# A fused attention and two feed-forward layers: five square groups on GpSimd, sums by rows first, the first fold in quarters

## The chip, the cores and the metric

The kernel runs on one core of a Trainium2 chip. The metric is device time in microseconds (us) from one launch to its end. Engines are named as in the profile: PE is TensorE (PEld its weight loads), DVE is VectorE, ACT is ScalarE, POOL is GpSimd, SP is SyncE, which here only issues DMAs.

## What is computed

```python
qn = q / (np.linalg.norm(q, axis=1, keepdims=True) + 1e-06)     # q, k, v: 1 x 6016 x 256, f32
kn = k / (np.linalg.norm(k, axis=1, keepdims=True) + 1e-06)
s = kn.transpose(0, 2, 1) @ qn / tau                            # 256 x 256
a = np.exp(s - s.max(-1, keepdims=True)); a /= a.sum(-1, keepdims=True) + 1e-09
x = v @ a                                                       # 6016 x 256
h = x @ w_in1;  x = (h * np.cos(h)) @ w_out1                    # d_ff = 2048, weights f64
h = x @ w_in2;  x = (h / (1 + np.exp(-h))) @ w_out2
```

The norms run over the 6016 tokens, so each of the 512 columns of q and k has one sum of squares. `v @ a @ w_in1` is computed as `v @ (a @ w_in1)`: the attention matrix is folded into the first weight, and v goes straight through the folded weight.

## The kernel before

**Opening.** q and k come in 25 groups (`GROUPS`: two of one chunk, 22 of two, one of one; a chunk is 128 tokens x 512 columns) into seven buffers, loaded by SP in order. For each group PE adds k^T q to the score matrix S, in two halves S[0] and S[1] (`emit_scores`, L617, two passes of 256 columns per chunk and half; four groups, `FINE`, go in another form at L606). ACT squares the group (L649). DVE adds the squares to `acc` (L666), a tile of two chunk rows x 512. The squares of the groups in `SIDE` = 7, 11, 15, 20 are added to a second tile, `aside`, by POOL (L661). Group 7 is squared into `aside` itself; the later ones of `SIDE` go through a tile `sq` in SBUF of which there is one (`SQ_BUFS` = 1); all other groups' squares go to two PSUM rooms by turns. At group 22 (`JOINED`) DVE adds `aside` to `acc` (L668). The last four groups (`LATE` = 4) do only S[0] in the loop; their S[1] follows later.

**Weights.** w_in1 and w_out1 come as f64, in pieces of 1 MB, and are decoded in steps that are named by two letters and put into the order by hand. The second letter is the weight (W: w_in1, O: w_out1), the first the step: `l` with W or alone loads, `a` and `b` take the magnitude (ACT, L345) and round the low word (`a` on ACT, L297; `b` on POOL, L299), `c` clamps and shifts (DVE, L304 and L312), `j` joins sign and low word (DVE, L318, then POOL, L321), `s` splits into two parts (ACT, L369, then POOL, L370). `FRONT` names the steps that follow a group of the opening: `lW aW` after 14, `cW` after 15, `jW` after 17. `AFTER` stands between the last group and the sums.

**Between.** Eight small products give the column sums of `acc` (two chunk rows x four column blocks, L675), one the sum of tau (L676). Then r = 1/(sqrt + 1e-6) (ACT L681, DVE L682 and on), the scaled identity `aside` (DVE L685, ACT L684), its spread over rows by PE (L691), copied by DVE to `rq` (L694), and for each half a of S: scale (DVE L699), maximum (DVE L702), exp (ACT L703), two transposes (PE L710), copy to `ET` (DVE L711). `THEN` puts the steps `jO s0` ahead of the spread. Steps of `v`: `V` and `lv` load its blocks 0 and 1, `s0` and `s1` split them (ACT L504), `v0` and `v1` make the low parts (POOL L507), `x0` and `x1` take maxima (DVE L442).

**First fold and turns.** `BEFORE` is the order after that: `f00` and `f01` (`fold_half`, PE L759) multiply a by the first two 256-column halves of w_in1, ACT (L767) and DVE (L771) split the result into `wa`, DVE takes its maximum (L433). Then 16 turns follow, units (block, pair of column tiles) of blocks 0 and 1: PE `h` (L854), ACT sine (L1213), DVE product `t` (L1216), ACT high part (L865), DVE low part (L869), PE output `o` (L882). A bound on |h|, from `largest` and `firsts` by a small product (L455) and two DVE steps (L464, L465, tile `smalls`; for block 2 L492 to L497), is the scale of the sine; after turns 4, 8, 12 and 15 it stands in the room that the next `h` takes. The other three folds (`f1` to `f3`, L741), their splits (`e`, `l`, L750 and L794), maxima (`w`, L475) and the decode steps are spread over the turns by `EARLY`.

Every engine runs its instructions in the order in which the program emits them.

Of the kernel before, what the change touches and what calls it, by code (L numbers as in the profile page):

```python
# [15 lines left out]
AF = mybir.ActivationFunctionType  # L16
ALU = mybir.AluOpType
# [3 lines left out]
P = 128  # L21
# [25 lines left out]
ASIDE = [("wo2", 5), ("wo2", 6), ("wo2", 7)]  # L47
GROUPS = [1, 1] + 22 * [2] + [1]
FIRST = 2
LATE = 4  # L50
REST = 2
TAU = 9
SQ_BUFS = 1
FINE = {5: 'v', 8: 'v', 10: 'v', 13: 'a'}
BEHIND = 3
WARM = (9, 0)

FRONT = {14: 'lW aW', 15: 'cW', 17: 'jW'}
AFTER = 'l V lv lW aO l lW cO'
THEN = ['', '', 'jO s0', '']  # L60
SIDE = [7, 11, 15, 20]
JOINED = 22
BEFORE = 'v0 s1 v1 T0 T1 bW rs f00 x0 l00 w00 f01 l01 w01 tb'
TURNS = 16
OPENED = 13
FORMING = {13: 'A0', 14: 'A1', 15: 'B0', 16: 'B1', 17: 'V', 18: 'V A2', 19: 'V', 20: 'B2 A3', 22: 'B3'}
# [5 lines left out]
    'outer': {  # L72
        0: 'x1 l', 1: 'aO', 2: 'cO p1 lW', 3: 'e1 l10 l11 p2 w10 w11', 4: 'l', 5: 'aO', 6: 'cO',
        7: 'e2 l20 l21 w20 w21', 9: 'aO', 10: 'cO', 11: 'e3 l30 l31 w30 w31',
    },
}
# [151 lines left out]
def direct(ctx, tc, qk, vT, tau, w_in1, w_out1, w_in2, w_out2, outT, dp, kept, within):  # L228
# [302 lines left out]
    for eng in (nc.sync, nc.scalar, nc.sync):  # L531
# [47 lines left out]
        "hW": lambda: W1.join((slice(0, 1), slice(1, 2))),  # L579
        "bO": WO1.begin,  # L580
        "aO": lambda: WO1.begin(low="act"),
        "cO": WO1.clamp,
        "jO": WO1.join,
        "sO": WO1.split,
# [11 lines left out]

    fine = {}

    def emit_scores(g, both=range(CH)):
        c0 = sum(GROUPS[:g])  # L600
        if g in fine:
            kinds = fine[g]
            for j in range(GROUPS[g]):
                for a in both:
                    for i, k in PASSES:
                        nc.tensor.matmul(  # L606
                            S[a],
                            kinds[i][:, j, 1, a * P : (a + 1) * P],
                            kinds[k][:, j, 0, :],
                            start=False,  # L610
                            stop=False,
                            skip_group_check=True,
                        )
            return
        for j in range(GROUPS[g]):
            for a in both:
                nc.tensor.matmul(  # L617
                    S[a],
                    tiles[g][:, j, 1, a * P : (a + 1) * P],
                    tiles[g][:, j, 0, :],  # L620
                    start=(c0 + j == 0),
                    stop=(c0 + j == NCK - 1),
                    skip_group_check=True,
                )

    for g, n in enumerate(GROUPS):
        c0 = sum(GROUPS[:g])
        if g == len(tiles):
            load_group(nc.sync)
        t = tiles[g]  # L630
        if g == 0:
            nc.vector.memset(ones, 1.0)
            nc.vector.memset(rtau, 0.0)
            nc.vector.memset(sums, 1e-9)
            make_identity(nc, ident)
            warm_up(N[:, :P], WARM[0])
        if g == TAU:
            nc.sync.dma_start(out=rtau[0:1], in_=tau)
        if g not in FINE:
            emit_scores(g, range(CH) if g < len(GROUPS) - LATE else (0,))  # L640
        if g - BEHIND in FINE:
            emit_scores(g - BEHIND)
        if g == SIDE[0]:
            sq = aside
        elif g in SIDE:
            sq = ep.tile([P, GMAX, 2 * C], F32, tag="sq", name=f"sq{g}", bufs=SQ_BUFS)
        else:
            sq = ps_hs[sum(i not in SIDE for i in range(g)) % 2].tile([P, GMAX, 2 * C], F32, tag="h", name=f"sq{g}")
        nc.scalar.activation(sq[:, :n], t[:, :n].rearrange("p g s d -> p g (s d)"), AF.Square)  # L649
        if g in FINE:  # L650
            k = len(fine)
            hi, lo = [w[k // 2][:, k % 2].rearrange("p j (s c) -> p j s c", s=2) for w in (wa, wo1)]
            fine[g] = (hi, lo)
            if FINE[g] == "a":
                nc.scalar.activation(hi, t, AF.Copy)
            else:
                nc.vector.tensor_scalar(out=hi, in0=t, scalar1=1.0, scalar2=1.0, op0=ALU.mult, op1=ALU.mult)
            nc.gpsimd.tensor_tensor(out=lo, in0=t, in1=hi.bitcast(F32), op=ALU.subtract)
        if g in SIDE:
            if g > SIDE[0]:  # L660
                nc.gpsimd.tensor_tensor(out=aside, in0=aside, in1=sq, op=ALU.add)  # L661
        elif c0 < GMAX:
            assert c0 + n <= GMAX
            nc.vector.tensor_copy(acc[:, c0 : c0 + n], sq[:, :n])
        else:
            nc.vector.tensor_tensor(out=acc[:, :n], in0=acc[:, :n], in1=sq[:, :n], op=ALU.add)  # L666
        if g == JOINED:
            nc.vector.tensor_tensor(out=acc, in0=acc, in1=aside, op=ALU.add)  # L668
        steps_of(FRONT.get(g, ""))
    steps_of(AFTER)  # L670

    for j in range(GMAX - 1, -1, -1):
        for i in range(2 * CH):
            st = dict(start=(j == GMAX - 1 and i == 0), stop=(j == 0), skip_group_check=True)
            nc.tensor.matmul(N[:, i : i + 1], acc[:, j, i * P : (i + 1) * P], ones[:, 0:1], **st)  # L675
    nc.tensor.matmul(N[:, 2 * CH : 2 * CH + 1], ones, rtau, start=False, stop=True, skip_group_check=True)  # L676
    steps_of(THEN[0])
    late = range(len(GROUPS) - LATE, len(GROUPS))
    for g in late[:REST]:
        emit_scores(g, (1,))  # L680
    nc.scalar.activation(r.rearrange("p s a -> p (s a)"), N[:, : 2 * CH], AF.Sqrt)  # L681
    nc.vector.tensor_scalar_add(r, r, 1e-6)  # L682
    nc.vector.reciprocal(r, r)
    nc.scalar.activation(aside[:, 0, :P], ident, AF.Copy, scale=r[:, 0, 0:1])  # L684
    nc.vector.tensor_scalar_mul(aside[:, 0, P:C], ident, r[:, 0, 1:2])  # L685
    nc.scalar.activation(warm, eps, AF.Exp)
    steps_of(THEN[1])
    nc.vector.reciprocal(rtau, N[:, 2 * CH : 2 * CH + 1])
    nc.vector.tensor_scalar_mul(r[:, 1], r[:, 1], rtau)
    steps_of(THEN[2])  # L690
    nc.tensor.matmul(N[:, C:], ones, aside[:, 0, :C], start=True, stop=True)  # L691
    for g in late[REST:]:
        emit_scores(g, (1,))
    nc.vector.tensor_copy(rq, N[:, C:])  # L694
    steps_of(THEN[3])


    for a in range(CH):
        nc.vector.scalar_tensor_tensor(  # L699
            out=E[:, a], in0=S[a], scalar=r[:, 1, a : a + 1], in1=rq, op0=ALU.mult, op1=ALU.mult  # L700
        )
        nc.vector.tensor_reduce(out=nmax[:, a : a + 1], in_=E[:, a], axis=AX.X, op=ALU.max, negate=True)  # L702
        nc.scalar.activation(  # L703
            E[:, a], E[:, a], AF.Exp, bias=nmax[:, a : a + 1], accum_out=sums[:, a, 0:1]
        )
    pts = [ps_hs[a].tile([P, 2, TB], F32, tag="h", name=f"pt{a}") for a in range(CH)]

    def emit_turn(a):
# [3 lines left out]
            ET[:, :, a * P : (a + 1) * P], pts[a][:, 0, : CH * P].rearrange("p (d c) -> p d c", d=CH)  # L712
        )

    warm_up(pts[0][:, 1, :P], WARM[1])

    def table():
        nc.scalar.activation(warm, eps, AF.Silu)
# [2 lines left out]
        nc.vector.tensor_reduce(out=rs, in_=sums, axis=AX.X, op=ALU.add)  # L721
        nc.vector.reciprocal(rs, rs)

    calls.update(T0=lambda: emit_turn(0), T1=lambda: emit_turn(1), tb=table, rs=inverse_sums)


    turn_of = [0]
# [23 lines left out]
            fold_to(j, a, 0), pws[j, a].rearrange("p (m f) -> p m f", m=2), AF.Copy, scale=rs[:, a : a + 1]  # L751
        )

    def fold_half(m):
        fold_room(0, m)
        for a in range(CH):
            pws[0, a] = pws[0, a][:, : TB // 2]
            for d in range(CH):
                nc.tensor.matmul(  # L759
                    pws[0, a],  # L760
                    ET[:, d, a * P : (a + 1) * P],
                    w1[:, d, m * TB // 2 : (m + 1) * TB // 2],
                    start=(d == 0),
                    stop=(d == CH - 1),
                )
        for a in range(CH):
            nc.scalar.activation(fold_to(0, a, 0)[:, m], pws[0, a], AF.Copy, scale=rs[:, a : a + 1])  # L767

    def fold_low_half(m):
        for a in range(CH):  # L770
            nc.vector.scalar_tensor_tensor(  # L771
                out=fold_to(0, a, 1)[:, m],
                in0=pws[0, a],
                scalar=rs[:, a : a + 1],
                in1=fold_to(0, a, 0)[:, m].bitcast(F32),
                op0=ALU.mult,
                op1=ALU.subtract,
            )
# [24 lines left out]
    for j in range(NF // 4):  # L803
        calls[f"f{j}"] = lambda j=j: fold_whole(j)
        calls[f"e{j}"] = lambda j=j: fold_highs(j)
        for a in range(CH):
            calls[f"f0{a}"] = lambda a=a: fold_half(a)
            calls[f"l{j}{a}"] = (lambda j=j, a=a: fold_low(j, a)) if j else (lambda a=a: fold_low_half(a))
            calls[f"w{j}{a}"] = (lambda j=j, a=a: span_of_weights(j, a)) if j else (lambda a=a: span_of_half(a))
    steps_of(BEFORE)  # L810
# [412 lines left out]
    for i, u in enumerate(units):  # L1223
# [16 lines left out]
        if i == 2:  # L1240
            ready.append(h_tile("bound2"))
            bound_piece(0, (b,), ready[0][:, 1])
        steps_of(EARLY["amid"].get(i, ""))
        if pend is not None and i != 2:
            emit_high(pend)
            if i != 3:
                emit_low(pend)
        steps_of(EARLY["inner"].get(i, ""))
        if i == TURNS + 6:
            bound(FIRST + 1, o1_room(FIRST + 1)[:, 0])  # L1250
        elif bounded:
            ready.append(h_tile(f"bound{i}"))
            if i < TURNS - 1:
                bound_piece(i // 4, range(FIRST), ready[0][:, 1])
            else:
                bound(FIRST, ready[0][:, 1])
        cosine_in(i, hp)
        if i == 2:
            emit_high(pend)
# [464 lines left out]
```

## Time and profile before

| | us |
|---|---|
| median of 3 runs | 992.57 (991.49 to 992.81) |
| profiled execution | 992.28 |
| its span, first to last instruction | 990.5 |
| PE busy | 981.6 |
| DVE busy | 820.2 |
| ACT busy | 785.3 |
| POOL busy | 403.0 |

The profile is one execution. Its timeline lists instructions by start; the chain of waits follows back from the last instruction what released each step. PE's ends are modelled and a waiting PE can look busy, so lost PE time is read from the starts of its products, not from its busy share. From here on a moment such as 40.9 is us from the start of the span.

### The profile page before, as it was taken

To read this page: it belongs to the slowest core of one execution; us is meant where nothing else is said; L and a number is where in the kernel's file an instruction comes from. 1 tells how busy PE (TensorE), PEld (TensorE's weight loads), DVE (VectorE), ACT (ScalarE), POOL (GpSimd) and SP (SyncE) were. 2 spreads that over 40 slices of the span, in tenths; PEclk is the share of its full clock that TensorE was granted. 3 is DMA by queue.
4 is the path that set the end of the run, shared out by engine and by line. 5 is a ranking of instruction groups with operands and counts; after the bars stand their busy time and mean duration, and the time that the engine had idled before them with its cause. 6 is when DMAs were issued, how large, how long until landed. Compare 5 with 4: busy or idle time off the path is not lost.

```text
span 990.5 us, 18764 instructions
## 1 busy us (share of the span) xinstructions
PE 981.6 (99%) x7092; PEld 930.0 (94%) x7092; DVE 820.2 (83%) x1290; ACT 785.3 (79%) x1443; POOL 403.0 (41%) x379
## 2 busy tenths in 40 slices
PE   9999999999999999999999999999999999999997
PEld 8877888899999999999999999999999999999997
DVE  6787778878788878788865889999999999999972
ACT  6776657688888888888876888888888888888863
POOL 5443368657768678777363111111111111111100
PEclk9999999999999999999999999999999999999999
DMA  9921025723433434333579722022022022021001
GB/s 374 375 90 64 1 106 214 255 87 138 138 139 129 160 122 166 130 137 134 189 296 385 293 76 96 13 86 97 12 86 94 15 86 83 26 86 53 29 12 40
DMA packets 35012, 126.59 MB, mean 128 GB/s; under 512 B 3170, under 2 KB 4450, under 8 KB 30178
## 3 DMA queue, kind: packets, MB, share of 16 engines
q1 hardware_dynamic: 34626, 124.86, 34.0%
q8 instruction: 57, 0.93, 0.4%
q10 hardware_dynamic: 288, 0.46, 0.1%
q14 instruction: 41, 0.34, 0.1%
HBM read 73.01 MB, written 52.30 MB: 127 GB/s over the span
## 4 chain that ended last, share of the span: by engine, by line
PE 94%; DVE 3%; ACT 2%; issue 1%; POOL 0%; ACTq 0%; DVEq 0%
PE o L1097 20%; PE xz L1097 20%; PE o L1461 17%; PE ys L1097 15%; PE o L882 6%; PE h L854 4%; PE S L617 3%; PE o L1137 2%; PE bound L854 1%; PE xz L1126 1%; PE ys L1126 1%; PE xz L1416 1%; PE ys L1416 1%; ACT t L1213 1%; PE pw L741 1%
## 5 line engine op out<-in xcount | busy, mean ns | idle before, releaser
L913 DVE TENSOR_TENSOR lo<-t,hi 128x768 fp32r<-128x768 f32 (+1 forms) x176 | 194.8, 1116 | 29.2 <-ACT hi L905 29.1
L900 POOL TENSOR_TENSOR t<-t 128x256 f32<-128x256 f32 x88 | 64.6, 734 | 356.6 <-DVE t L897 300.9
L905 ACT ACTIVATE hi<-t 128x768 fp32r<-128x768 f32 (+1 forms) x176 | 168.6, 958 | 26.8 <-PE o L1097 25.9
L1461 PE MATMUL o<-hi,wo 128*128 128x512 f32 x512 | 142.0, 380 | 0.0
L1097 PE MATMUL o<-hi,wo 128*128 128x256 f32 x770 | 134.7, 275 | 0.0
L1097 PEld LDWEIGHTS o<-hi,wo 128*128 128x128 f32 x770 | 117.1, 192 | 0.0
L1097 PE MATMUL o<-lo,wo 128*128 128x256 f32 x385 | 105.9, 275 | 0.0
L1461 PEld LDWEIGHTS o<-hi,wo 128*128 128x128 f32 x512 | 87.4, 190 | 6.8
L1515 DVE TENSOR_TENSOR xz<-xz,t 128x512 f32<-128x512 f32 x64 | 44.7, 698 | 42.1 <-ACT t L1509 41.1
L1461 PE MATMUL o<-lo,wo 128*128 128x512 f32 x256 | 76.1, 380 | 0.0
L1097 PEld LDWEIGHTS ys<-xhi,wf 128*128 128x128 f32 x384 | 67.7, 190 | 7.2 <-ACT u L1552 0.4
L1097 PE MATMUL ys<-xhi,wf 128*128 128x256 f32 x384 | 74.2, 275 | 0.2 <-ACT u L1552 0.2
L1097 PEld LDWEIGHTS o<-lo,wo 128*128 128x128 f32 x385 | 73.9, 192 | 0.0
L1097 PE MATMUL xz<-xhi,wa 128*128 128x256 f32 x384 | 71.8, 276 | 0.0
L1620 ACT ACTIVATE ys<-xz 128x256 f32<-128x256 f32 x88 | 32.4, 368 | 45.9 <-PE xz L1097 44.9
L1097 PEld LDWEIGHTS xz<-xhi,wa 128*128 128x128 f32 x384 | 62.9, 191 | 3.4
L1097 PE MATMUL xz<-x2hi,wf 128*128 128x256 f32 x352 | 65.8, 275 | 0.0
L1097 PE MATMUL xz<-x2hi,wa 128*128 128x256 f32 x352 | 65.8, 275 | 0.0
L882 PE MATMUL o<-hi,wo 128*128 128x512 f32 (+1 forms) x256 | 60.5, 373 | 0.0
L892 DVE TENSOR_TENSOR t<-t 128x512 f32<-128x512 f32 x88 | 60.3, 685 | 0.1
L1650 ACT ACTIVATE t<-t 128x512 f32<-128x512 f32 x88 | 55.6, 632 | 2.3 <-DVE t L1147 2.1
L1506 ACT ACTIVATE ys<-xz 128x256 f32<-128x256 f32 x64 | 23.6, 368 | 39.9 <-PE xz L1097 38.7
(287 smaller groups left out, 3155.3 us busy)
## 6 DMA issues: line engine op xcount, KB each, us to landing
qk<-qk_dram SPq DMA_DIRECT2D x22, 512.0 KB, 6.1
x2hi<-xshi SPq DMA_DIRECT2D x11, 896.0 KB, 4.9
x2lo<-xslo SPq DMA_DIRECT2D x11, 896.0 KB, 7.3
wi_dram<-stage SPq DMA_DIRECT2D x8, 1024.0 KB, 3.8
wo_dram<-stage SPq DMA_DIRECT2D x8, 1024.0 KB, 4.5
outT_dram<-q SPq DMA_DIRECT2D x22, 256.0 KB, 2.0
vraw<-vT_dram SPq DMA_DIRECT2D x10, 512.0 KB, 4.0
xshi<-t SPq DMA_DIRECT2D x10, 512.0 KB, 5.4
```

The source lines that it names most:

```text
L617: nc.tensor.matmul(S[a], tiles[g][:, j, 1, a * P : (a + 1) * P], tiles[g][:, j, 0, :], start=(c0 + j == 0), stop=(c0 + j == NCK - 1), skip ...
L854: nc.tensor.matmul(hp[:, s, :n], wa_at(i, a, 2 * m + s), columns(x[k][:, a, :n]), start=((i, k) == passes[0] and a == 0), stop=((i, k) == ...
L882: nc.tensor.matmul(o[:, e, :n], wo1_at(i, f)[:, e * P : (e + 1) * P], columns(parts[k][:, s, :n]), start=(f == 0 and (i, k) == PASSES[0]), ...
L892: eng.tensor_tensor(out=t[:, 4:6, :c], in0=t[:, 0:1, :c].to_broadcast([P, 2, c]), in1=t[:, 1:3, :c], op=ALU.subtract)
L900: eng.tensor_tensor(out=t[:, 7, :c], in0=t[:, 3, :c], in1=t[:, 6, :c], op=ALU.subtract)
L905: nc.scalar.activation(hi[:, sl, :c], t[:, 1:][:, sl, :c], AF.Copy)
L913: nc.vector.tensor_tensor(out=lo[:, sl, :c], in0=t[:, 1:][:, sl, :c], in1=hi[:, sl, :c].bitcast(F32), op=ALU.subtract)
L1097: nc.tensor.matmul(out, w(p, ka), columns(x[r][:, kb - 1]), start=(start and i == 0), stop=(stop and i == 2), skip_group_check=True,)
L1461: nc.tensor.matmul(o[:, e], wo1_at(i, f)[:, e * P : (e + 1) * P], columns(parts[k][:, s]), start=(f == 0 and (i, k) == PASSES[0]), stop=(f ...
L1515: nc.vector.tensor_tensor(out=xz[k], in0=xz[k], in1=sines[:, 1], op=ALU.mult)
L1620: nc.scalar.activation(y2, x2, AF.Copy)
L1650: nc.scalar.activation(t[:, 0:2], t[:, 0:2], AF.Silu)
```

## The change

It makes `SIDE` 7, 11, 15, 18, 20 and adds, after group 20, one POOL addition of `aside`'s second row to its first. The join moves to group 23 and becomes two DVE additions of 512 columns, so that the sums need four products; the product of tau goes ahead of them. `LATE` is 5, and the late S[1] products are counted by chunks, three of nine ahead of the spread of r. One load of w_out1 goes ahead of groups 23 and 24. `s0` moves from the middle of the scaling to `AFTER`. The two halves of S are no longer handled in one loop: `bW` comes after the first exp, the first transposes before the second maximum. The first fold is cut into four quarters, those of S's first half ahead of the second's, and the high parts of each half follow. In the turns `p1` goes ahead of `cO`, one round of the low word moves from turn 5 to turn 6, and the bounds of turns 4 and 15 move ahead of the decode steps and of the high and low parts. `WARM` and `THEN` lose entries that were empty.

```diff
-LATE = 4
-REST = 2
+LATE = 5
+REST = 3
+AMID = 'jO'
-FRONT = {14: 'lW aW', 15: 'cW', 17: 'jW'}
-AFTER = 'l V lv lW aO l lW cO'
-THEN = ['', '', 'jO s0', '']
-SIDE = [7, 11, 15, 20]
-JOINED = 22
-BEFORE = 'v0 s1 v1 T0 T1 bW rs f00 x0 l00 w00 f01 l01 w01 tb'
+FRONT = {14: 'lW aW', 15: 'cW', 17: 'jW', 22: 'l'}
+AFTER = 'V lv lW aO l lW s0 cO'
+SIDE = [7, 11, 15, 18, 20]
+JOINED = 23
+BEFORE = 'v0 s1 v1 q00 T1 q10 rs q01 h0 q11 x0 l00 w00 h1 l01 w01 tb'
...
-        0: 'x1 l', 1: 'aO', 2: 'cO p1 lW', 3: 'e1 l10 l11 p2 w10 w11', 4: 'l', 5: 'aO', 6: 'cO',
+        0: 'x1 l', 1: 'aO', 2: 'p1 cO lW', 3: 'e1 l10 l11 p2 w10 w11', 4: 'l', 5: 'dO', 6: 'rO cO',
...
+        "dO": lambda: WO1.begin(low=False),
+        "rO": lambda: WO1.round_low(WO1.begun[0][1], True),
...
                 nc.gpsimd.tensor_tensor(out=aside, in0=aside, in1=sq, op=ALU.add)
+            if g == SIDE[-1]:
+                nc.gpsimd.tensor_tensor(out=aside[:, 0], in0=aside[:, 0], in1=aside[:, 1], op=ALU.add)
...
         if g == JOINED:
-            nc.vector.tensor_tensor(out=acc, in0=acc, in1=aside, op=ALU.add)
+            for more in (aside[:, 0], acc[:, 1]):
+                nc.vector.tensor_tensor(out=acc[:, 0], in0=acc[:, 0], in1=more, op=ALU.add)
...
-    for j in range(GMAX - 1, -1, -1):
-        for i in range(2 * CH):
-            st = dict(start=(j == GMAX - 1 and i == 0), stop=(j == 0), skip_group_check=True)
-            nc.tensor.matmul(N[:, i : i + 1], acc[:, j, i * P : (i + 1) * P], ones[:, 0:1], **st)
-    nc.tensor.matmul(N[:, 2 * CH : 2 * CH + 1], ones, rtau, start=False, stop=True, skip_group_check=True)
+    small_sum = dict(stop=True, skip_group_check=True)
+    nc.tensor.matmul(N[:, 2 * CH : 2 * CH + 1], ones, rtau, start=True, **small_sum)
+    for i in range(2 * CH):
+        nc.tensor.matmul(N[:, i : i + 1], acc[:, 0, i * P : (i + 1) * P], ones[:, 0:1], start=False, **small_sum)
+    late = [(g, j) for g in range(len(GROUPS) - LATE, len(GROUPS)) for j in range(GROUPS[g])]
+    for g, j in late[:REST]:
+        emit_scores(g, (1,), (j,))
...
-    for a in range(CH):
...
+    scaled(0)
+    maxima(0)
+    exponential(0)
+    steps_of("bW")
+    scaled(1)
+    emit_turn(0)
+    maxima(1)
+    exponential(1)
...
+    def fold_quarter(m, a):
+        if a == 0:
+            fold_room(0, m)
+            pw_halves[m] = [pws[0, i][:, : TB // 2] for i in range(CH)]
+        for d in range(CH):
+            nc.tensor.matmul(
+                pw_halves[m][a],
+                ET[:, d, a * P : (a + 1) * P],
+                w1[:, d, m * TB // 2 : (m + 1) * TB // 2],
+                start=(d == 0),
+                stop=(d == CH - 1),
+            )
...
         steps_of(EARLY["amid"].get(i, ""))
+        if i in (4, TURNS - 1):
+            ready.append(h_tile(f"bound{i}"))
+        if i == TURNS - 1:
+            bound(FIRST, ready[0][:, 1])
         if pend is not None and i != 2:
             emit_high(pend)
             if i != 3:
                 emit_low(pend)
+        if i == 4:
+            bound_piece(1, range(FIRST), ready[0][:, 1])
```

## Rows read from the trace of the kernel before

**Rows 1.** The page, part 4: shares of the chain that ended last.

```profile
PE 94%; DVE 3%; ACT 2%; issue 1%; POOL 0%; ACTq 0%; DVEq 0%
```

**Rows 2.** Timeline of PE, 26 to 56: start, us, engine, line, tiles, shape, count, idle.

```profile
31.44 10.09 PE L617 MATMUL S<-qk 128*128 128x256 f32 x46
41.37 1.84 PE L675 MATMUL S<-ones,acc 128*128 128x1 f32 x16
...
45.54 1.46 PE L617 MATMUL S<-qk 128*128 128x256 f32 x6
47.85 0.44 PE L710 MATMUL pt<-ident,E 128*128 128x128 f32 x2 [0.85 <-ACT E L703]
...
52.24 0.78 PE L854 MATMUL h<-xhi,wa 128*128 128x512 f32 x2
```

**Rows 3.** Timeline of ACT, 26 to 47.

```profile
26.63 2.90 ACT L649 ACTIVATE sq<-qk 128x1024 f32<-128x1024 f32 x3
...
31.20 2.01 ACT L649 ACTIVATE sq<-qk 128x1024 f32<-128x1024 f32 x2 [0.30 <-DVE acc L666]
...
40.97 1.13 ACT L345 ACTIVATE wv_wo<-raw_wo 128x1024 f32<-128x1024 f32 x1 [2.90 <-DMA raw_wo<-w_out_dram]
```

**Rows 4.** Timeline of POOL, 26 to 47.

```profile
27.75 2.37 POOL L661 TENSOR_TENSOR aside<-aside,sq 128x1024 f32<-128x1024 f32 x1 [2.98 <-ACT sq L649]
32.41 2.42 POOL L321 TENSOR_TENSOR w<-w,raw_w 128x1024 int32<-128x1024 int32 x1 [2.29 <-DVE w L318]
34.77 2.39 POOL L661 TENSOR_TENSOR aside<-aside,sq 128x1024 f32<-128x1024 f32 x1
```

**Rows 5.** Timeline of DVE, 26 to 47.

```profile
31.08 1.25 DVE L318 SCALAR_TENSOR_TENSOR w<-raw_w,w 128x1024 int32<-128x1024 int32 x1
32.22 5.21 DVE L666 TENSOR_TENSOR acc<-acc,sq 128x1024 f32<-128x1024 f32 x4
37.53 1.23 DVE L668 TENSOR_TENSOR acc<-acc,aside 128x1024 f32<-128x1024 f32 x1
38.86 2.01 DVE L666 TENSOR_TENSOR acc<-acc,sq 128x1024 f32<-128x1024 f32 x2
42.13 0.69 DVE L304 TENSOR_SCALAR wv_wo<-wv_wo 128x1024 f32<-128x1024 f32 x1 [1.25 <-ACT wv_wo L345]
42.86 0.69 DVE L312 TENSOR_SCALAR wv_wo<-wv_wo 128x1024 int32<-128x1024 int32 x1
```

**Rows 6.** The chain that ended last, 41 to 54: start, us, what.

```profile
43.68 0.18 DVE r L682
...
45.85 0.34 DVE rq L694
...
48.04 0.61 ACT E L703 x2
```

**Rows 7.** Waits of PE's weight loads, 50 to 150: us, times, longest.

```profile
PEld bound L854 <- ACT wf L1077: 1.0, 1, 1.0
PEld bound L854 <- DVE smalls L465: 0.8, 2, 0.5
PEld h L854 <- DVE wa L794: 0.8, 2, 0.5
PEld h L854 <- ACT wa L750: 0.4, 1, 0.4
```

**Rows 8.** Timeline of PE, 140 to 146.

```profile
144.03 1.10 PE L854 MATMUL bound<-xhi,wa 128*128 128x512 f32 x4 [0.58 <-DVE smalls L497]
```

**Rows 9.** Timeline of PE, its first rows and its last one.

```profile
1.09 4.05 PE L595 MATMUL S<-ones 128*128 128x128 f32 x18 [1.09 <-DVE sums L634]
...
984.90 0.49 PE L1137 MATMUL o<-lo,wo 128*128 128x384 f32 x2
```

**Rows 10.** Windows: busy time by engine, then granted clock, DMA share, GB/s.

```profile
20.00:30.00 10.00, 10.00 (x59) 9.14 (x57) 5.80 (x7) 7.65 (x9) 7.02 (x4) 1.00 1.03 418
...
988.00:990.50 2.50, 0.00 (x0) 0.00 (x0) 0.00 (x0) 0.00 (x0) 0.00 (x0) 0.50 0.04 10
```

More of the change, by code (lines that the diff above doesn't have):

```diff
@@ L55 @@
 BEHIND = 3
-WARM = (9, 0)
-FRONT = {14: 'lW aW', 15: 'cW', 17: 'jW'}
-AFTER = 'l V lv lW aO l lW cO'
-THEN = ['', '', 'jO s0', '']
-SIDE = [7, 11, 15, 20]
-JOINED = 22
-BEFORE = 'v0 s1 v1 T0 T1 bW rs f00 x0 l00 w00 f01 l01 w01 tb'
+WARM = 9
+FRONT = {14: 'lW aW', 15: 'cW', 17: 'jW', 22: 'l'}
[3 more added lines that the diff above has]
+BEFORE = 'v0 s1 v1 q00 T1 q10 rs q01 h0 q11 x0 l00 w00 h1 l01 w01 tb'
 TURNS = 16
@@ L597, in direct, with emit_scores @@
     fine = {}
-    def emit_scores(g, both=range(CH)):
+    def emit_scores(g, both=range(CH), chunks=range(GMAX)):
         c0 = sum(GROUPS[:g])
@@ L614, in emit_scores @@
             return
-        for j in range(GROUPS[g]):
+        for j in chunks[: GROUPS[g]]:
             for a in both:
@@ L635, in direct @@
             make_identity(nc, ident)
-            warm_up(N[:, :P], WARM[0])
+            warm_up(N[:, :P], WARM)
         if g == TAU:
@@ L667, in direct @@
         if g == JOINED:
-            nc.vector.tensor_tensor(out=acc, in0=acc, in1=aside, op=ALU.add)
+            for more in (aside[:, 0], acc[:, 1]):
+                nc.vector.tensor_tensor(out=acc[:, 0], in0=acc[:, 0], in1=more, op=ALU.add)
         steps_of(FRONT.get(g, ""))
     steps_of(AFTER)
-    for j in range(GMAX - 1, -1, -1):
-        for i in range(2 * CH):
-            st = dict(start=(j == GMAX - 1 and i == 0), stop=(j == 0), skip_group_check=True)
-            nc.tensor.matmul(N[:, i : i + 1], acc[:, j, i * P : (i + 1) * P], ones[:, 0:1], **st)
-    nc.tensor.matmul(N[:, 2 * CH : 2 * CH + 1], ones, rtau, start=False, stop=True, skip_group_check=True)
[L677 to L680, printed above, removed]
+    small_sum = dict(stop=True, skip_group_check=True)
[5 more added lines that the diff above has]
+        emit_scores(g, (1,), (j,))
     nc.scalar.activation(r.rearrange("p s a -> p (s a)"), N[:, : 2 * CH], AF.Sqrt)
@@ L686, in direct, with scaled @@
     nc.scalar.activation(warm, eps, AF.Exp)
-    steps_of(THEN[1])
     nc.vector.reciprocal(rtau, N[:, 2 * CH : 2 * CH + 1])
     nc.vector.tensor_scalar_mul(r[:, 1], r[:, 1], rtau)
-    steps_of(THEN[2])
+    steps_of(AMID)
     nc.tensor.matmul(N[:, C:], ones, aside[:, 0, :C], start=True, stop=True)
-    for g in late[REST:]:
-        emit_scores(g, (1,))
+    for g, j in late[REST:]:
+        emit_scores(g, (1,), (j,))
     nc.vector.tensor_copy(rq, N[:, C:])
-    steps_of(THEN[3])
-    for a in range(CH):
+    def scaled(a):
         nc.vector.scalar_tensor_tensor(
@@ L701, in direct, with maxima, exponential @@
         )
+    def maxima(a):
         nc.vector.tensor_reduce(out=nmax[:, a : a + 1], in_=E[:, a], axis=AX.X, op=ALU.max, negate=True)
-        nc.scalar.activation(
-            E[:, a], E[:, a], AF.Exp, bias=nmax[:, a : a + 1], accum_out=sums[:, a, 0:1]
-        )
+    def exponential(a):
+        nc.scalar.activation(E[:, a], E[:, a], AF.Exp, bias=nmax[:, a : a + 1], accum_out=sums[:, a, 0:1])
     pts = [ps_hs[a].tile([P, 2, TB], F32, tag="h", name=f"pt{a}") for a in range(CH)]
@@ L713, in emit_turn @@
         )
-    warm_up(pts[0][:, 1, :P], WARM[1])
+    scaled(0)
[6 more added lines that the diff above has]
+    exponential(1)
     def table():
@@ L722, in inverse_sums @@
         nc.vector.reciprocal(rs, rs)
-    calls.update(T0=lambda: emit_turn(0), T1=lambda: emit_turn(1), tb=table, rs=inverse_sums)
+    calls.update(T1=lambda: emit_turn(1), tb=table, rs=inverse_sums)
     turn_of = [0]
@@ L752, in fold_high, with fold_high_half @@
         )
-    def fold_half(m):
-        fold_room(0, m)
-        for a in range(CH):
[L757 to L767, printed above, removed]
+    pw_halves = {}
+    def fold_quarter(m, a):
[10 more added lines that the diff above has]
+            )
+    def fold_high_half(m):
+        for a in range(CH):
+            nc.scalar.activation(fold_to(0, a, 0)[:, m], pw_halves[m][a], AF.Copy, scale=rs[:, a : a + 1])
     def fold_low_half(m):
@@ L772, in fold_low_half @@
                 out=fold_to(0, a, 1)[:, m],
-                in0=pws[0, a],
+                in0=pw_halves[m][a],
                 scalar=rs[:, a : a + 1],
@@ L806, in direct @@
         for a in range(CH):
-            calls[f"f0{a}"] = lambda a=a: fold_half(a)
+            calls[f"h{a}"] = lambda a=a: fold_high_half(a)
+            for m in range(2):
+                calls[f"q{m}{a}"] = lambda m=m, a=a: fold_quarter(m, a)
             calls[f"l{j}{a}"] = (lambda j=j, a=a: fold_low(j, a)) if j else (lambda a=a: fold_low_half(a))
@@ L1250, in direct @@
             bound(FIRST + 1, o1_room(FIRST + 1)[:, 0])
-        elif bounded:
+        elif i in (8, 12):
             ready.append(h_tile(f"bound{i}"))
[L1253 to L1256, printed above, removed]
+            bound_piece(i // 4, range(FIRST), ready[0][:, 1])
         cosine_in(i, hp)
```

## Prediction

> **What bounds the kernel now.** Read the chain first: 94% of it is PE [rows 1], so an edit is worth what it changes in PE's work or in the time that PE stands still. Then PE's timeline where the change lies. From 31.44 the scores run without a hole: 46 passes in the 9.93 us up to 41.37 are 0.216 us each, against 0.213 for 256 columns of four-byte data at the pace of that stretch [rows 2]. The 46 are four whole groups (17 to 20, eight passes each) and the S[0] halves of 21 to 24 (fourteen). DVE ends its last addition at 40.87 (38.86 + 2.01) [rows 5]. So two things end together at about 41: PE's scores and the squares' sums. A change must pull both. After that comes a chain of short steps, in which PE loses about 1.6 us around the two transposes: it stands from 46.8 to 47.85 and 0.4 us again before the second pair [rows 2]; the first product of the turns starts at 52.24. From there to 150 the weight loads wait 3.0 us in all [rows 7], of which the products feel about six tenths (at 144.03 the load waited 1.0 and the product 0.58 [rows 7, 8]): 1.8 us that orders in the turns can give back. Behind that PE is full.
>
> **Five groups on GpSimd.** This edit decides. The rows give the order of three engines. ACT squares 15, 16 and 17 from 26.63, and 19 and 20 from 31.20 [rows 3]. POOL adds 15 at 27.75 to 30.12, then waits for DVE's join of w_in1 (31.08 to 32.33), adds the low word at 32.41 to 34.82 and adds group 20 at 34.77 to 37.16 [rows 4, 5]; DVE's own join with `aside` starts at 37.53, right behind [rows 5]. POOL is thus full from 32.41 on. Group 18's addition comes after the decode step in program order, so it takes the place of group 20's: 34.77 to 37.16. The new thing is the buffer. Groups 11, 15, 18 and 20 are squared into the one `sq`, so ACT can't square 20 before POOL has added 18: at 37.18 instead of about 32.2. Queued behind that square on ACT are the squares of 21 to 24, and for those DVE waits.
>
> From there, step by step, with 0.96 us from one square to the next (2.90 less one square of 1.03, halved, is 0.94 [rows 3]) and 1.23 us an addition with 0.10 between two [rows 5]: squares 20, 21, 22 start at 37.18, 38.14, 39.09; DVE adds 21 at 39.20 to 40.42 and 22 at 40.52 to 41.75. Square 23 needs the PSUM room that 21's addition frees: 40.45; its addition ends at 43.07. Square 24, half as long, needs 22's room: 41.78 to 42.4. POOL adds 20 at 38.3 to 40.7, and its row addition (half of 2.39, 1.2) ends at 41.9, before DVE needs it. The two joins take 0.68 each (2.01 less 1.23 and a gap [rows 5]), 43.17 to 44.65, and group 24 ends at **45.44**, against 40.87: +4.57, although DVE adds one group less.
>
> **The late halves.** A fifth late group takes four passes from PE's loop: it ends 0.85 earlier, at about 40.5. That is no gain, since the sums come next in PE's queue and the nine late chunks stand behind them: PE is idle from 40.6 to 45.5.
>
> **Rows first, tau first.** Eight products are 16 passes in 41.37 to 43.07 (0.106 each; the tau pair starts there); half of them saves 0.85 and tau's pair 0.2. The sums are ready at 45.5 + 0.85 + 0.15 = 46.5. DVE, however, has the clamp and shift (`cO`, 2 x 0.69 and a gap, 1.42 [rows 5]) between its last addition and r: until 46.87. So r begins at 46.87 against 43.68 [rows 6]: +3.2.
>
> **w_out1's load, `aO`, `s0`.** The 1 MB takes 2.5 us at 418 GB/s [rows 10], and groups 23 and 24 land up to 2.5 later. Cost taken: nothing, because both are squared after 40.4 only, and PE, should it wait for their scores, waits inside its idle time up to 45.5; were that cover gone, up to 2.5 us. In return ACT no longer waits for it (2.90 now [rows 3]): the magnitude, the round and `s0`'s copy (about 1.15 each) run from 42.4 to 45.6, before the root needs ACT at 46.5.
>
> **Scaling, quarters, `bW`.** From r to the copy of `rq` the steps are the same, 2.17 us (43.68 to 45.85, with the join `jO` in it [rows 6]): 49.0. PE's three late chunks fit ahead of it (six passes, 1.28, from 46.4; then the spread). The six chunks behind take 2.58 and end at 51.0, so DVE scales S[1] at 51.0. The steps that follow are short ones (two transposes 0.44 [rows 2], exp 0.61 [rows 6], the others up to 0.5 each): scale and copy of `ET` take it to 51.9, the first two quarters (four passes each, 0.86) run around the second transposes, and the last two end at 55.7. ACT's step of `bW`, a magnitude of about 1.15 (1.13 [rows 3]), lies between the exps while DVE copies and takes the second maximum; its round on POOL (at most the 2.4 of the adds [rows 4]) goes ahead of `v0`, which behind it ends at about 55.7 to 56.4, when `h` wants it: 0 to 0.7, taken as 0. The first `h` follows at 55.7 without the 0.2 that it loses now, and the turns stand at **+3.3 us**. Counted on PE alone: 5.0 idle, less 0.9 of products, less 2.0 of holes closed, plus 1.2 of new holes between the six chunks and the last quarters.
>
> **The turns.** `p1` ahead of `cO` frees the sine's tile earlier, and with it the third turn's fold parts (0.8 + 0.4 of load waits [rows 7]); the two bounds moved up meet the 0.5 and the 1.0. Moving one round to turn 6 clears ACT there. Bounds: nothing, and the whole 1.8; I take all four steps as working, at **-1.8**, and the lower end for the range.
>
> **The clock.** PE has no hole in this trace as long as the 4.9 us. The rows that show a change of level: at the start 18 passes of 128 columns take 4.05 us, twice what 128 columns take later (half of 0.213), so PE starts at 1.2 GHz and is at 2.4 after about 4 us of work; at the end PE stops at 985.4, and from 988.0 the granted clock is 0.50 [rows 9, 10]. A stop of 2.6 us was enough there, so I expect 1.2 GHz when the sums begin, for about the 4 us of the start, and half of that lost: **+1.9** (bounds 0 and 4: no fall, or all late chunks and sums at the low level). The Trainium skill says this too (TensorE: Matmul & The Clock Gate, "Why this matters for your kernels": idle gaps between bursts of matmuls send the array back to half clock); the trace agrees at its end, and by the rule no step of the sum changes.
>
> **Sum.** 992.28 (profiled; 0.29 under the median) + 3.3 + 1.9 - 1.8 = 995.7. The empty entries of `WARM` and `THEN` are worth nothing.
>
> **Rivals.**
> *The clock holds.* Idle of 4.9 us leaves it at 2.4 GHz: 992.28 + 3.3 - 1.8 = 993.8, which a measurement can't tell from no change. For it: nothing but that no idle in mid-kernel is there to see. 0.18.
> *POOL isn't the limit, and it gets faster.* Place: group 18's addition. If it is done by about 32.2, ahead of or beside the decode step, the square of 20 keeps its time; then DVE, with one addition less, ends near 40.9, PE's sums start there, 0.9 of products and some 1.5 of holes go, 1.2 come: -1.2, and with the turns 992.28 - 1.2 - 1.8 = 989.3. It decides from the moment at which the sums' last addition ends before some 42. Against it: both POOL rows are 2.4 us and in order. Between, where 23's late landing sets the end (43), it gives 991.4. 0.10 for both.
> *Low clock for longer, and nothing back in the turns.* 992.28 + 3.3 + 3 = 998.6; for it, that DVE's steps part PE's work after the stop, unlike at the start, and that the turns then wait elsewhere. 0.20.
> *The forecast* has 0.52.
>
> **How the numbers follow.** Predicted 995.7. The range leaves out about 0.10 below (the second rival and a little of the first) and 0.10 above: 992.8 to 998.4. About 0.2% (2.0 us) is what a measurement can tell from no change, so slower means above 994.6. Faster: the part of the second rival below 990.6, 0.07. Same: the first rival, the rest of the second, and the forecast's lower tail where the clock costs under 0.8: 0.25. Slower: 0.68.
>
> **What would show it.** ACT idle before group 20's square until POOL has added 18, about 5 us; DVE's last addition at 45.4; PE without a product from 40.6 to 45.5; passes of 256 columns at 0.427 after it; r at 46.9 or later; the first `h` at 55.7 (full clock) to 58; no waits on `wa` and `smalls` in turns 3, 4 and 16. The forecast is wrong if that square starts near 32, and too high if the passes after the stop keep 0.213.

## The result and the profile after

The changed kernel takes 997.87 us (median of 6 runs, 997.21 to 999.06) against 992.04 for the kernel before beside it: 1.0058 times as long, 95% interval 1.0047 to 1.0068. The profiled execution took 998.18 us, with a span of 996.2.

The first product of the turns starts at 59.45 instead of 52.24 [rows 2], 7.2 us later; from there to the end of the span it is 936.75 us instead of 938.26, 1.5 less. These two make the 5.7 us by which the span grew. The loss lies in the opening, then, and the turns give something back.

The chain that ended last tells why. Its columns are start, us and what, as in [rows 6].

```profile
31.34 1.15 DVE w L318
32.48 0.07 issue
32.55 2.40 POOL w L321
34.95 2.32 POOL aside L663
37.27 0.02 issue
37.30 0.02 ACT sq L651
...
39.30 1.23 DVE acc L670
```

In the kernel before, PE's scores carry the chain here, and POOL has 0% of it [rows 1]. Now the join of w_in1 on DVE (L318) releases POOL's part of it (L321), behind it POOL adds group 18 (L663), and only then ACT squares group 20 (L651). ACT's and DVE's timelines show what that wait holds up:

```profile
30.33 1.98 ACT L651 ACTIVATE sq<-qk 128x1024 f32<-128x1024 f32 x2 [0.62 <-POOL aside L663]
37.30 2.92 ACT L651 ACTIVATE sq<-qk 128x1024 f32<-128x1024 f32 x3 [4.99 <-POOL aside L663]
```

```profile
32.39 1.22 DVE L670 TENSOR_TENSOR acc<-acc,sq 128x1024 f32<-128x1024 f32 x1
39.30 3.87 DVE L670 TENSOR_TENSOR acc<-acc,sq 128x1024 f32<-128x1024 f32 x3 [5.70 <-ACT sq L651]
...
44.80 0.69 DVE L670 TENSOR_TENSOR acc<-acc,sq 128x512 f32<-128x512 f32 x1
...
47.65 0.17 DVE L685 TENSOR_SCALAR r<-r 128x4 f32<-128x4 f32 x1 [0.83 <-ACT r L684]
```

The row at 30.33 holds groups 18 and 19, the one at 37.30 groups 20 to 22. ACT is idle for 4.99 us before group 20, and DVE for 5.70 us before group 21. The last addition ends at 45.49; before it was 40.87 [rows 5]. PE's timeline and the granted clock by windows (the third number from the end of each row) show what follows:

```profile
40.86 0.28 PE L678 MATMUL S<-rtau,ones 128*128 128x1 f32 x2
45.55 1.87 PE L680 MATMUL S<-ones,acc 128*128 128x1 f32 x8 [4.41 <-DVE acc L670]
47.27 2.91 PE L619 MATMUL S<-qk 128*128 128x256 f32 x6
49.97 1.06 PE L693 MATMUL S<-aside,ones 128*128 128x256 f32 x2
50.83 4.01 PE L619 MATMUL S<-qk 128*128 128x256 f32 x12
54.68 0.38 PE L713 MATMUL pt<-ident,E 128*128 128x128 f32 x2
...
59.45 0.85 PE L870 MATMUL h<-xhi,wa 128*128 128x512 f32 x2
```

```profile
41.00:43.10 2.10, 0.14 (x3) 0.05 (x1) 2.00 (x2) 1.80 (x3) 1.16 (x1) 1.00 0.97 370
43.20:45.50 2.30, 0.00 (x0) 0.00 (x0) 2.08 (x4) 2.30 (x3) 0.00 (x0) 0.50 1.02 381
45.50:53.30 7.80, 7.75 (x22) 6.59 (x23) 4.68 (x11) 2.92 (x8) 3.25 (x2) 0.50 0.37 148
53.40:59.40 6.00, 5.31 (x27) 4.26 (x25) 2.91 (x7) 2.88 (x6) 4.16 (x3) 1.00 0.50 174
```

PE stands for 4.41 us. During the stop its clock falls from 2.4 to 1.2 GHz, and it stays there up to 53.4, 7.8 us into the work that follows. The starts of the late passes lie 0.427 us apart up to 53.38 and 0.216 behind it. So the six ahead of the spread take 0.45 us each on the mean and the twelve behind it, between 50.83 and 54.68, 0.32.

In the turns the waits of PE's weight loads, which were 3.0 us in four lines [rows 7], read so in the changed kernel (60 to 157):

```profile
PEld o L898 <- POOL wo L370: 0.9, 1, 0.9
PEld bound L870 <- DVE smalls L465: 0.3, 1, 0.3
PEld L455 <- DVE largest L433: 0.3, 1, 0.3
```

The waits on the fold's parts and the long one on the bound of turn 16 are gone. The one on POOL's split of w_out1 has grown: in the kernel before it stands below the four lines of [rows 7], in the same view, as

```profile
PEld o L882 <- POOL wo L370: 0.2, 1, 0.2
```

### The profile page after: what moved, and what is told of

Read it like the earlier page. It is cut to its first block, busy times and chain, and to the rows that moved or that the text cites. A ratio compares the mean times of both kernels' runs of the same rounds, so it can differ in the third digit from the quotient of the medians.

```text
span 996.2 us, 18750 instructions
## 1 busy us (share of the span) xinstructions
PE 983.9 (99%) x7084; PEld 932.6 (94%) x7084; DVE 819.4 (82%) x1290; ACT 785.5 (79%) x1443; POOL 408.2 (41%) x381
## 4 chain that ended last, share of the span: by engine, by line
PE 93%; issue 2%; DVE 2%; POOL 1%; DMA 1%; ACT 1%; SPq 0%; DVEq 0%; POOLq 0%; ACTq 0%
PE xz L1113 20%; PE o L1113 20%; PE o L1480 17%; PE ys L1113 15%; PE o L898 7%; PE h L870 4%; PE S L619 2%; PE o L1153 2%; PE bound L870 1%; DMA raw_w<-w_in_dram 1%; PE pw L751 1%; PE xz L1142 1%; PE ys L1142 1%; PE ys L1435 1%; PE xz L1435 1%
## 5 line engine op out<-in xcount | busy, mean ns | idle before, releaser
L1534 DVE TENSOR_TENSOR xz<-xz,t 128x512 f32<-128x512 f32 x64 | 44.7, 698 | 42.2 <-ACT t L1528 41.3
```

The source lines that it names most:

```text
L1534: nc.vector.tensor_tensor(out=xz[k], in0=xz[k], in1=sines[:, 1], op=ALU.mult)
```

## Experiments

### A second buffer

Group 20's squares get a tile of their own, which the decode doesn't use at that time.

```diff
-            sq = ep.tile([P, GMAX, 2 * C], F32, tag="sq", name=f"sq{g}", bufs=SQ_BUFS)
+            if g == SIDE[-1]:
+                sq = io.tile([P, NS * P], F32, tag="wv", name=f"sq{g}").rearrange("p (g c) -> p g c", g=GMAX)
+            else:
+                sq = ep.tile([P, GMAX, 2 * C], F32, tag="sq", name=f"sq{g}", bufs=SQ_BUFS)
```

> The changed kernel with a second buffer for group 20's squares alone (an idle decode tile), all else as changed. Theory A (the one buffer holds ACT, and with it DVE and PE): ACT squares 20 near 32.3 instead of 37.3, 21 and 22 follow; POOL still adds 18 and 20 behind the decode step and ends its row addition near 40.9; the squares' sums end near 43 (joins behind POOL and behind group 23, which lands near 38.4), 2.4 us earlier than 45.5; PE stands 2.2 us instead of 4.7. If a stop that short leaves the clock at 2.4 GHz, the 3.5 us of the low clock go too: 992 us. If it doesn't, 995.5. Rival B (POOL's additional work alone is the delay, whatever the buffers): sums end near 45, time near 997.5.

It took 996.31 us (995.01 to 997.35), 1.0043 of before (1.0028 to 1.0059). ACT's timeline and one row of PE's:

```profile
30.75 2.96 ACT L654 ACTIVATE sq<-qk 128x1024 f32<-128x1024 f32 x3 [0.62 <-POOL aside L666]
...
39.41 1.55 ACT L654 ACTIVATE sq<-qk 128x1024 f32<-128x1024 f32 x2 [3.29 <-DMA qk<-qk_dram]
```

```profile
44.06 1.80 PE L683 MATMUL S<-ones,acc 128*128 128x1 f32 x8 [2.41 <-DVE acc L673]
```

Groups 18 to 20 are now squared in one run, and PE's stop falls from 4.41 to 2.41 us, near theory A's 2.2. The buffer was the cause of ACT's 5 us. But the sums still end at 44.0, only 1.5 us earlier than in the changed kernel: what ends the squares then is group 23, which stands behind the w_out1 load and lands 3.29 us after ACT wants it. The clock fell all the same, from 44.2 to 51.0, so the time is near that of the second case of the expectation (995.5).

### Four groups on GpSimd, with and without work in PE's stop

```diff
-SIDE = [7, 11, 15, 18, 20]
+SIDE = [7, 11, 15, 20]
```

> The changed kernel with group 18 given back to DVE: SIDE is 7, 11, 15, 20, all else as changed. Theory A: ACT doesn't stand before group 20's square; DVE adds 18 to 22 without a hole by 37.6; then group 23, behind the w_out1 load, lands near 38.4 and sets the end: added by 40.7, joins by 42.1, group 24 by 42.9. PE stands 2 us, and if the clock holds the time is 992, as with two buffers. Rival C (the earlier load or the order of the scaling is what costs): sums' end near 43, but r and the first product of the turns as late as in the changed kernel, time near 997.

995.74 us, 1.0031 of before (1.0019 to 1.0044); seven of ten runs lie between 995.5 and 997.2, three between 992.3 and 993.5. In the profiled one the squares' sums end at 43.7, 0.8 later than expected (its w_in1 piece landed 0.5 later than in the changed kernel). PE stops for 2.53 us and the windows show:

```profile
43.75 1.87 PE L680 MATMUL S<-ones,acc 128*128 128x1 f32 x8 [2.53 <-DVE acc L670]
```

```profile
41.00:43.20 2.20, 0.22 (x3) 0.14 (x1) 1.96 (x4) 2.20 (x3) 0.00 (x0) 1.00 1.00 394
43.30:50.00 6.70, 6.25 (x19) 5.35 (x20) 4.49 (x11) 2.50 (x5) 1.78 (x1) 0.50 0.82 313
```

The mean granted clock that is on record for each run tells the two clumps apart: 0.995 or 0.996 in the seven long runs, 0.998 or 0.999 in the three short ones. So the fifth group on GpSimd isn't all of it: without it PE still stops long enough for the clock to fall in most runs. ACT waits 2.56 us for group 23, behind the earlier w_out1 load, and the fifth late group ends PE's loop four passes (0.86 us) earlier; what each does alone to the clock was not tried. The next kernel puts work into that stop.

```diff
-SIDE = [7, 11, 15, 18, 20]
+SIDE = [7, 11, 15, 20]
...
+    warm_up(N[:, :P], 12)
     small_sum = dict(stop=True, skip_group_check=True)
```

> side_four with 12 products of ones into the unused sums' room ahead of tau's product, 2.6 us of work in the 2.8 us in which PE waits; nothing that is used changes. Theory A (side_four's runs lie in two clumps, 992.3 to 993.5 and 995.5 to 997.2, because the stop of 2.8 us lowers the clock in most executions and not in all): clock 1.00 throughout, r at 45.1, first product of the turns near 54.0, all runs within 0.5 us of 992.6. Rival F (the clumps have another cause, such as landings): again two clumps, median near 995.5.

992.64 us (992.09 to 993.73 in ten runs), 1.000 of before (0.9991 to 1.0009):

```profile
43.10:53.20 10.10, 9.58 (x51) 7.76 (x49) 7.52 (x18) 5.90 (x13) 6.30 (x4) 1.00 0.70 266
```

No run is near 995.5, though they spread wider than the 0.5 us expected, and the granted clock is at 1.00 from the start's rise to PE's end. Theory A holds: the two clumps were the clock. Its price is 3.1 us between the medians of these two kernels, and 3.6 between the medians of the two clumps of the first (996.15 and 992.51).

### PE kept at work in the changed kernel

```diff
+    warm_up(N[:, :P], 22)
     small_sum = dict(stop=True, skip_group_check=True)
```

> The changed kernel with 22 products of ones into the unused sums' room ahead of tau's product, so that PE works (4.7 us at full pace) through the time in which it waits for the squares; nothing that is used changes. Theory A: DVE's last addition stays at 45.5, granted clock 1.00 throughout, passes of the late scores 0.213 instead of 0.427, and 3.5 us less: 994.4. Rival D (the low clock costs little, since DVE and ACT set the pace between the sums and the turns): 997 to 998.

994.78 us (994.41 to 995.71), 1.003 of before (1.0018 to 1.0042). PE's timeline, and a window:

```profile
40.27 5.07 PE L597 MATMUL S<-ones 128*128 128x128 f32 x44
45.19 0.28 PE L679 MATMUL S<-rtau,ones 128*128 128x1 f32 x2
45.55 1.05 PE L681 MATMUL S<-ones,acc 128*128 128x1 f32 x8
46.47 1.54 PE L619 MATMUL S<-qk 128*128 128x256 f32 x6
47.84 0.65 PE L694 MATMUL S<-aside,ones 128*128 128x256 f32 x2
48.34 2.75 PE L619 MATMUL S<-qk 128*128 128x256 f32 x12
51.02 0.44 PE L714 MATMUL pt<-ident,E 128*128 128x128 f32 x2
...
55.69 0.85 PE L871 MATMUL h<-xhi,wa 128*128 128x512 f32 x2
```

```profile
45.00:53.00 8.00, 7.37 (x41) 5.83 (x39) 6.24 (x15) 5.06 (x11) 3.68 (x3) 1.00 0.44 170
```

DVE's last addition stays at 45.5, but each stretch of PE behind it is shorter than in the changed kernel: from the first sum to the late passes 0.92 us instead of 1.72, the six passes 1.37 instead of 2.70, the spread 0.50 instead of 0.86, the twelve 2.68 instead of 3.85. Together 3.7 us, and the first product of the turns comes 3.76 earlier. In the medians it is 3.1. That is what the low clock cost; rival D falls.

### The orders in the turns alone

The kernel before, with the changed entries of `EARLY` for turns 2, 5 and 6 and the earlier bounds of turns 4 and 15, as the diff of the change shows them.

> The kernel before with nothing but the changed orders in the turns (low part of turn 1 ahead of the clamp, one round moved from turn 5 to 6, bounds of turns 4 and 15 moved up). Theory A: 1.5 us less than before, 990.5, without PE's waits on the third turn's fold parts and on the bounds of turns 4 and 16. Rival E (in the changed kernel the turns gained only because they began later, with the decode ahead of them): within 0.3 us of before.

990.90 us (990.56 to 992.01, 11 runs) against 992.01: 0.9991 of before, interval 0.9982 to 1.0000. From the first product of the turns to the end of the span it is 936.76 us, as in the changed kernel (936.75) and 1.5 less than before (938.26); in all nine profiles with the changed turns it is 936.7 to 937.3. By the profiles the gain of the turns is their own, and rival E falls; in the medians it is 1.1 us, at the edge of what the interval can tell from none. The loads' waits between 50 and 150 are nearly those of the changed kernel too:

```profile
PEld o L884 <- POOL wo L370: 0.9, 1, 0.9
...
PEld bound L856 <- DVE smalls L465: 0.3, 1, 0.3
```

The wait on POOL's split has grown because PE comes earlier: its weight loads are ready for w_out1's part at 85.66 instead of 86.95, 1.3 us earlier, while POOL's split ends only 0.65 earlier (86.46 instead of 87.11).

### Four late groups

The filled kernel, with one late group less and 18 products of ones instead of 22.

```diff
-LATE = 5
+LATE = 4
...
+    warm_up(N[:, :P], 18)
     small_sum = dict(stop=True, skip_group_check=True)
```

> filled with four late groups in place of five (18 products of ones, since PE's loop ends 0.85 later; three late chunks ahead of the spread as in the changed kernel, four behind it). Theory A (the fifth late group buys nothing while the squares set the end, and its two chunks stand ahead of the second half's scaling): first product of the turns 0.7 us earlier, 994.1 against filled's 994.8. Rival G (late chunks fill holes that PE would have anyway): the same as filled, or slower.

994.57 us (994.14 to 995.87), 1.0021 of before (1.0011 to 1.0031), where the filled kernel has 1.0030 (1.0018 to 1.0042). The two were timed beside different runs of before (992.55 and 992.01), and the intervals overlap: the times can't tell 0.7 us less from nothing. The profile can: the first product of the turns is at 55.78, in the filled kernel at 55.69. Theory A's part on the late chunks falls:

```profile
48.45 1.89 PE L619 MATMUL S<-qk 128*128 128x256 f32 x8
51.13 0.44 PE L714 MATMUL pt<-ident,E 128*128 128x128 f32 x2 [0.79 <-ACT E L708]
```

With four passes less PE reaches the transposes earlier and waits there for the first exp. The two extra chunks lie in a hole that is there anyway, as rival G had it.

### The decode step behind the additions

Five groups and five late ones, but w_in1's join behind POOL's two additions, and w_out1's load and `s0` where they were.

```diff
-FRONT = {14: 'lW aW', 15: 'cW', 17: 'jW', 22: 'l'}
-AFTER = 'V lv lW aO l lW s0 cO'
+FRONT = {14: 'lW aW', 15: 'cW', 20: 'jW'}
+AFTER = 'l V lv lW aO l lW cO'
...
-AMID = 'jO'
+AMID = 'jO s0'
```

> The changed kernel, five groups on GpSimd and five late ones, with two orders undone or moved: w_out1's load behind group 24 and s0 in the middle of the scaling, as before, and the join of w_in1 after group 20, behind POOL's additions of 18 and 20. Theory A (a decode step ahead of POOL's additions, then group 23's landing, are all that made the squares late): ACT squares 20 near 34, no landing later than 37.5, the squares' sums end near 41.3, PE has no stop, clock 1.00, r near 43.8 (the w_out1 piece lands near 41 again and its clamp and shift set r), first product of the turns near 52.6, 991.3. Rival H (five groups are too many for POOL in any order): sums' end 43 or later, a stop of 2 us or more, 993 to 996.

995.65 us (994.44 to 996.68), 1.0029 of before (1.0019 to 1.0039). ACT squares group 20 at 34.54, near the 34 expected, and no landing holds the squares. But the sums end at 43.84. DVE's timeline, POOL's and PE's:

```profile
40.53 1.79 DVE L673 TENSOR_TENSOR acc<-acc,aside 128x512 f32<-128x512 f32 x1
42.36 0.69 DVE L673 TENSOR_TENSOR acc<-acc 128x512 f32<-128x512 f32 x1
```

```profile
39.36 2.41 POOL L321 TENSOR_TENSOR w<-w,raw_w 128x1024 int32<-128x1024 int32 x1
```

```profile
43.89 1.87 PE L680 MATMUL S<-ones,acc 128*128 128x1 f32 x8 [2.68 <-DVE acc L670]
```

The first join takes 1.79 us instead of 0.69. It starts beside POOL's join, which ends at 41.78, and it ends 0.55 after that, as if it had stood until POOL was done. The rest is that group 20's square at 34.54 still comes 2.4 us later than in the kernel before (32.16), with 21 to 24 behind it on ACT; 0.8 of that is the w_in1 piece, which ACT takes at 25.37 in this profile and at 24.54 in the one before. PE stops for 2.7 us, the clock falls (0.996 or 0.997 over each of the nine runs), and the time is in the place of rival H. Its mechanism isn't shown: without the 1.1 us that DVE stood, the sums would have ended near 42.7. Theory A's 41.3 was too early in any case: from square 20 to the sums' end it is 8.2 us without that wait, which from 34 makes 42.2. Whether five groups would do with the decode step further back was not tried.

### The changed scaling and quarters behind the old opening

The changed kernel with the opening of the kernel before: `SIDE`, `JOINED`, one join, eight products, `FRONT`, `AFTER`, `s0` in the middle of the scaling, `LATE` = 4 and four late chunks ahead of the spread. New against before are tau's product ahead of the sums, the order from the scaling on and the turns.

> The kernel before up to the squares' sums (four groups on GpSimd, one join, eight products, w_out1 behind group 24, four late groups, four chunks ahead of the spread, three behind), with the changed order from the scaling on: tau first, bW between the exps, first transposes ahead of the second maximum, quarters, and the changed turns. Theory A: r at 43.6 as before, six steps less in line behind it, first product of the turns near 51.7, 990.4, 0.5 less than with the turns alone. Rival I (the quarters' order only moves holes, as the first product 8.8 us behind r in filled against 8.6 before suggests): 991 to 991.2.

991.78 us (991.12 to 992.72) against 992.55 beside it: 0.9995 of before (0.9986 to 1.0004), against 0.9991 with the turns alone. The order of the scaling adds nothing that the intervals can tell. From r to the first product of the turns it is 8.82 us (44.45 to 53.27), in the kernel before 8.56 (43.68 to 52.24). DVE's timeline:

```profile
47.84 0.47 DVE L698 SCALAR_TENSOR_TENSOR E<-S,r,rq 128x256 f32<-128x256 f32 x1
49.09 0.43 DVE L713 COPY ET<-pt 128x256 f32<-128x256 f32 x1 [0.78 <-PE pt L712]
49.43 0.41 DVE L703 TENSOR_REDUCE nmax<-E 128x1 f32<-128x256 f32 x1
```

The second maximum stands behind the first copy of `ET` on DVE, which waits 0.78 us for PE. So the second exp and transposes come later by about what the quarters save, as rival I had it.

## Why the prediction was right

**The one buffer.** Right within 0.15 us, step by step: square 20 at 37.30 (37.18 forecast), POOL's addition of 20 at 38.43 to 40.81 (38.3 to 40.7), the last addition to 45.49 (45.44). PE stands from 41.1 to 45.5 (40.6 to 45.5). The second buffer shows that ACT's wait was the buffer's. The forecast's other limit, group 23's late landing at an end near 43, is what came next in that run and with four groups.

**The sum at full clock.** r at 46.87 and the first product at 55.7 were forecast. The filled kernel has 46.85 and 55.69. So the terms of the opening but the clock hold together as they stood, the cover of w_out1's load by PE's idle time among them. Two details inside that sum need a correction. That the late chunks set the second scaling is so in the timeline, but taking two away changed nothing, since PE then waits for the exp. And the 0.2 us that the forecast took off behind the first product are still lost there (0.69 us from its first pair of passes to the second, 0.62 before, 0.43 further on): so it is +3.45 and not +3.3.

**The clock.** Right in sign, too small in size: this is the term that was mis-sized. Forecast was +1.9 us, half of a stretch at the low level that lasts for about 4 us of work, as at the start. The halving was right: passes start 0.427 us apart, as forecast, against 0.216 at the high level. The length was wrong: the level stayed low for 7.8 us of work and cost 3.1 (medians) to 3.8 us (profiles), near the upper bound of 4. The step that failed is the transfer from one start. In the ten profiles the trace's clock record begins with the rise, 3.1 to 5.5 us behind PE's first product, so even the start has no one length. (Ahead of the record the view by windows shows 1.00; the low level is read there from the passes of 128 columns, 0.216 us each against 0.112 in the filled kernel's stop.) Why the level stayed low for longer behind the stop is not shown: from 45.55 to 53.38 PE's passes start one behind the other without a hole, so breaks in PE's work, the reason that the third rival gave, are not to be seen there. Rival 1 (the clock holds) took a stop of 4.9 us for possible without a fall. The clock fell in all six runs of the changed kernel (0.994 to 0.996 over the run), and stops of 2.4 to 2.7 us were enough in most or all runs of three other kernels.

The third rival, the low clock for longer and nothing back in the turns (998.6, at 0.20), lies nearer to 997.87 than the forecast does. Its first half came, with 3.8 us where it had 3; its second didn't.

**The turns.** -1.8 was forecast, taking all steps as working. It was -1.5 in the profile. The third turn's and the two bounds' waits went as described; what was not foreseen is that the wait on POOL's split of w_out1, 0.2 us in the kernel before, grows to 0.9 when PE comes earlier, and takes some of it back.

**The total.** 3.3 + 1.9 - 1.8 gave 995.7; measured terms are 3.45 + 3.76 - 1.51 = +5.7 on the span. The distance of 2.2 us from the forecast to 997.87 is mostly the clock's 1.9. All three terms erred to the same side, so nothing cancelled. The later start of the turns, 7.2 us, can be split by the profiles of two kernels in which PE was kept at work: 3.8 are the clock, 2.4 the fifth group on GpSimd (55.69 in the filled kernel, 53.25 with four groups), and 1.0 the rest of the opening's changes (53.25 against 52.24).

The rival in which POOL isn't the limit falls by its own condition: group 18's addition ran from 34.91 to 37.26 and was not done by 32.2. Its middle case, an end near 43 set by group 23's late landing, is what the second buffer and the four groups show (44.0 and 43.7). But those took 996.31 and 995.74 us and not 991.4: the rival had no fall of the clock in it. With PE kept at work the four groups took 992.64.

## What to carry to other kernels

Before work is moved to an engine with time to spare, follow its queue at that very moment, and the buffers that it will hold: a single buffer turns a helper's backlog into a stop of the engine that fills it and of all that is queued there. And where PE is the bound, price a stop twice: its length, and the low clock behind it. The turns' orders alone are the part of this change worth keeping (0.9991 of before, interval up to 1.0000).

## What the runs showed of the hardware

- PE's granted clock fell with a stop of 2.41 us (second buffer, in all four runs by the clock on record for each) and of 2.68 us (decode step behind the additions, in all nine); with four groups on GpSimd and a stop of 2.53 us it fell in seven runs of ten. In these three profiles it stayed at 0.50 for 6.8 us, and after it fell in the stop of 4.41 us for 10.2 (43.1 to 53.4), of which 7.8 were work. The Trainium skill (TensorE: Matmul & The Clock Gate, "Why this matters for your kernels") names idle gaps of PE between bursts of matmuls as what drops the throughput in mid-kernel; the trace agrees that gaps do it, with stops of 2.41 and 4.41 us, but the first of them is shorter than the gap that the section still allows, and here the measurement decides.
- A DVE addition with both inputs in SBUF that started beside a POOL instruction took 1.79 us instead of 0.69 and ended 0.55 us behind it. The additions of `acc`, whose second input is in PSUM, ran at 1.22 to 1.24 us beside POOL's work (at 32 to 37 in the kernel before). The Trainium skill (SBUF — State Buffer, "SBUF: two separate sides") says that a DVE operation with two SBUF inputs and a GpSimd operation that reads SBUF take a shared pair of ports in turn, for a whole instruction each; the trace agrees, with the 1.79 us.
